# Fused attention, top-1 experts and gated feed-forward: a rare-case branch moved behind the feed-forward, the limits in one transfer, more TensorE fillers, another VectorE order

## The chip, the cores and the metric

The kernel runs on one core of a Trainium2 chip. The metric is the device time of one execution in microseconds (us); each kernel is run several times and the median is given. The engines are TensorE (PE in the profile; PEld is its weight load), VectorE (DVE), ScalarE (ACT), GpSimd (POOL) and SyncE (SP, which here only issues transfers). A name with q at its end (POOLq) is an engine's instruction sequencer.

## What is computed

Three stages, in float32, on B = 2 sequences of S = 768 tokens, H = 8 heads of D = 64 (cut from the reference):

```python
scores = scale * np.matmul(q, k.transpose(0, 1, 3, 2))
keep = is_sink | in_window             # key < n_sink, or 0 <= query - key < window
a = np.exp(scores - max); a = a / (sum + 1e-09); x = np.matmul(a, v)   # -> x[1536, 512]
logits = xn @ en.T / tau               # both normed; 8 experts
expert_idx = argmax(logits); gate_w = softmax(logits)[expert_idx]
x[mask] = gate_w[mask, None] * (np.maximum(x[mask] @ w1[e], 0.0) @ w2[e])   # F = 1024
out = ((x @ w_a) * (x @ w_b)) @ w_out  # d_ff = 1536
```

`n_sink` is 4 and `window` is 128, both given as 64-bit integers at run time.

## The kernel before

All products are made to float32 accuracy from three float32r products: an operand is split into a high part (a cast on ScalarE or VectorE) and the rest (a subtraction on VectorE), and hi*hi, lo*hi and hi*lo are added in PSUM. The kernel writes its instruction order by hand (`tc.manual_schedule()`): every engine runs its instructions in the order in which the program's lines issue them, and waits where a tile is not ready.

**Start and attention.** SP issues the first halves of q and k, then the two limits (lines 193 and 194, each broadcast to 128 partitions into `ctli`), then the second halves and further loads. VectorE turns the limits into masks (`early_masks`, lines 222 to 229) before it can use the first scores (`sc_exp`, line 474). A loop over g goes through the 12 token tiles, four steps each (one step: two heads): `p_t` transposes the weights of two steps ago, `sc_mm` makes scores (line 459 for the first tile, 465 for the others), `pv` multiplies by v, `back` and what follows finish a tile and route it to an expert. While little real work is there, `warm_pe(n)` issues n transposes of the identity into a PSUM tile that nobody reads (line 964), the fillers: `WARM` = 8 + 4 + 3 ahead of the first scores, and `WARMG[g]` at the end of step g.

**Experts.** Tokens are sorted by expert; weights are loaded by expert and split; items of one or two tiles of tokens run through `mm1`/`mm2` and `pa`/`pb` (lines 708, 780 to 782, 800 to 802) and their results go to `y_d` in DRAM (`ys`, line 768). In the same loop the gate values, the position of every token and the counts `cnt` are worked out a few instructions at a time (`side_gen`), and the feed-forward's weights begin to be decoded.

**The branch.** A plan with a fixed number of slots covers the usual case. If the limits or the counts don't fit it, a general path repairs the result: line 1473 loads a count into a register of each engine, line 1475 compares it, and the repair (a thousand PE instructions) is jumped over when the count is 0, as it is here. The jumped path has a short block of its own, in which every engine waits until its earlier work and transfers are done and raises its semaphores by what the repair would have added. Then comes the feed-forward.

**Feed-forward.** Tokens go in NG = 3 groups of 512, the 1536 hidden units in NF = 12 steps f of 128. For each f, `ab_mms` makes 24 products for a and b (lines 1600 to 1602), `g_split` multiplies them (`asb`, line 1609), splits the result into `gh` (ScalarE, 1612) and `gl` (VectorE, 1613), and `out_mms` makes 12 products into four PSUM tiles (1620 to 1622), one step later. The weights arrive packed and are decoded in 24 halves: `conv_step(m)` casts the high part of half m on ScalarE, and on VectorE prepares half m+1 (`conv_b0`, two operations, lines 1384 and 1385; `conv_b1`, two, lines 1390 and 1391) and subtracts the low part of m (`wl`, line 1401). Four halves are decoded before the first group, the other 20 during its steps f = 0 to 9, one `conv_step` ahead of `g_split` and one behind it:

```python
        ab = ab_mms(f)
        if more:
            conv_step(2 * (f + NF0), f1)
        cur = g_split(f, ab, 'V')
        if more:
            conv_step(2 * (f + NF0) + 1, f1)
```

`done` scales a finished tile and scatters its rows to the output with an indirect transfer from POOL (line 1667). At the program's end (line 1721) SP waits for every transfer, and all engines meet.

Of the kernel before, what the change touches and what calls it, by code (L numbers as in the profile page):

```python
# [20 lines left out]
P = 128  # L21
# [42 lines left out]
WARMG = [6, 3, 4, 1]  # L64
# [38 lines left out]
TINY = 2.0 ** -15 * 1.125  # L103

# [19 lines left out]
def tile_kernel(ctx, tc, q, k, v, n_sink, window, emb, tau, w1, w2, wc, out, dbg=None):  # L124
# [1046 lines left out]
    fe = pool(ctx, "fe", side="right")  # L1171

    def side_gen(w_, pl, psp, tag):
# [172 lines left out]
        V.tensor_copy(cide, cpos[:, 0:4])  # L1346
        G.tensor_scalar(g, g, 1.0 / GSC, None, op0=ALU.mult)
# [16 lines left out]
    wres = {}  # L1364

    raw2, sq2 = {}, {}
# [3 lines left out]
    def load_conv(m):  # L1370
        if m >= NH:
            return
        r = raw2[m] = fe.tile([P, HW, 2], I32, tag="raw", name="raw2", bufs=3)
        nc.sync.dma_start(r.rearrange("p n c -> p (n c)"), wc32[m])

    def conv_abs(m):
        if m < NH:
            sq2[m] = fe.tile([P, HW], F32, tag="sq", name="sq", bufs=2)
            nc.scalar.activation(sq2[m], raw2[m][:, :, 1].bitcast(F32), AF.Abs)  # L1379

    def conv_b0(m):
        if m < NH:
            b, t = sq2[m], sq2[m].bitcast(I32)
            nc.vector.tensor_scalar(b, b, TINY, None, op0=ALU.max)  # L1384
            nc.vector.tensor_scalar(t, t, 5, 2, op0=ALU.logical_shift_left, op1=ALU.logical_shift_right)

    def conv_b1(m):
        if m < NH:
            r, t = raw2.pop(m), sq2[m].bitcast(I32)
            nc.vector.scalar_tensor_tensor(t, r[:, :, 0], 29, t, op0=ALU.logical_shift_right, op1=ALU.bitwise_or)  # L1390
            nc.vector.scalar_tensor_tensor(t, r[:, :, 1], -1073741824, t, op0=ALU.bitwise_and, op1=ALU.bitwise_or)  # L1391

    def conv_step(m, wpool):
        f, h = divmod(m, 2)
        if h == 0:
            wres[f] = (wpool.tile([P, CW], F32R, name=f"wh{f}"), wpool.tile([P, CW], F32R, name=f"wl{f}"))
        wh, wl = (t[:, h * HW:(h + 1) * HW] for t in wres[f])
        sq = sq2.pop(m)
        nc.scalar.copy(wh, sq)
        conv_b0(m + 1)  # L1400
        nc.vector.tensor_tensor(out=wl, in0=sq, in1=wh, op=ALU.subtract)  # L1401
        conv_abs(m + 2)
        conv_b1(m + 1)
        load_conv(m + 4)

    xh2 = fe.tile([P, NP, TG], F32R, name="xh2")
    xl2 = fe.tile([P, NP, TG], F32R, name="xl2")
    ygs = {}

    def gather_y(u, w=None, rows=None):  # L1410
        ygs[u] = w.tile([P, DM], F32, tag="ygn", name="ygn", bufs=4) if w else fe.tile([P, DM], F32, tag="yg", name="yg", bufs=3)
        early = u < 4 and w is None
        nc.gpsimd.indirect_dma_start(out=ygs[u], out_offset=None, in_=y_d[0:rows or (YR0 if early else YR1), :],  # L1413
                                     in_offset=bass.IndirectOffsetOnAxis(ap=(cide if early else cidx)[:, u:u + 1], axis=0))

    def y_t(u, psp, tag):
        yp = psp.tile([P, NP, P], F32, tag=tag, name="yp2")
        for kc in range(NP):
            nc.tensor.transpose(yp[:, kc, :], ygs[u][:, kc * P:(kc + 1) * P], ident)  # L1419
        return yp  # L1420

    def y_s(u, yp):
        tt = u % 4
        ts_ = slice(tt * P, (tt + 1) * P)
        nc.scalar.copy(xh2[:, :, ts_], yp)
        nc.vector.tensor_tensor(out=xl2[:, :, ts_], in0=yp, in1=xh2[:, :, ts_], op=ALU.subtract)
# [46 lines left out]
    ns_v = nc.values_load(cnt[0:1, 0:1], min_val=0, max_val=4 * int(GENF))  # L1473
    mst.close()
    with tc.If(ns_v > 0):  # L1475
# [97 lines left out]
        with ExitStack() as gs:  # L1573
            xw = pool(gs, "xw3")
            xps = pool(gs, "xps3", space=PSUM)
            for u in range(NU):
                gather_y(u, xw, NBLK * P)
                nc.sync.dma_start(y2_d[u * P:(u + 1) * P, :], ygs[u])
            for u in range(NU):
                yc = xw.tile([P, DM], F32, tag="ygn", name="yc", bufs=4)  # L1580
                nc.sync.dma_start(yc, y2_d[u * P:(u + 1) * P, :])
                nc.sync.dma_start(y_d[u * P:(u + 1) * P, :], yc)
            nc.vector.tensor_copy(cidx, tok)
            for u in range(4):
                gather_y(u, xw, YR1)
                y_s(u, y_t(u, xps, "a"))
# [29 lines left out]
    def out_mms(po, f, gh, gl, done=None, tts=range(4)):  # L1616
        wh, wl = wres[f]
        for tt in tts:
# [4 lines left out]
            if done is not None:  # L1623
                done(tt)

    NG = NT // TG
    outs = []
    pend = None
    tail = []
# [95 lines left out]
```

## Time and profile before

| | |
|---|---|
| median of 3 runs | 661.46 us (661.29 to 661.57) |
| the profiled execution, its own time | 659.85 us |
| its span, first to last instruction | 658.0 us |
| PE busy | 628.6 us, 96% of the span |
| PEld busy | 515.4 us, 78% |
| DVE busy | 396.4 us, 60% |
| ACT busy | 304.8 us, 46% |
| POOL busy | 122.2 us, 19% |
| mean granted TensorE clock | 0.977 of full speed |

The page divides the span into 40 slices; in its line for the clock only the first two slices, slice 21, near 335 us, and the last stand clearly below full. The stretches show the same by stage. Busy shares are means over stages with different limits: attention to about 100 us, experts to 329 us, the first feed-forward group to 430 us, the other two to the end. In the timeline a row gives the start in us, the duration in us (of several equal instructions together, with their count), engine, line, operation, the tile written and the tiles read, and in brackets how long the engine had been idle and what ended that.

### The profile page before, as it was taken

How to read it: one execution, taken by the hardware profiler on the slowest of the kernel's cores; microseconds unless marked ns; L12 is line 12 of the kernel's file. 1: busy time of each engine (PE TensorE's matmuls, PEld its weight loads, DVE VectorE, ACT ScalarE, POOL GpSimd, SP SyncE). 2: the span in 40 equal slices, each digit the busy share in tenths (PEclk: the TensorE clock that was granted, in tenths of full speed). 3: DMA queues.
4: the chain of work that ended last, by engine and by line, in shares of the span. 5: the costliest groups of instructions: out<-in, count | busy, mean ns of one | idle time of the engine just before them, and what ended most of it. 6: DMA issues, size and time to landing. Idle time of an engine off the chain costs nothing. (4 is left out here: it accounts for less than half of the span.)

```text
span 658.0 us, 10420 instructions
## 1 busy us (share of the span) xinstructions
PE 628.6 (96%) x3665; PEld 515.4 (78%) x3665; DVE 396.4 (60%) x910; ACT 304.8 (46%) x581; POOL 122.2 (19%) x269
## 2 busy tenths in 40 slices
PE   8999999889999999998969999999999999999995
PEld 5777777779998989887858767678888888888884
DVE  5688878998888766798839999943111113111111
ACT  4678777667575657667524444422111113111111
POOL 7243345481042211020010000004000003000002
PEclk7699999989999999999979999999999999999999
DMA  4244325323787887587253454203000002000001
GB/s 144 85 160 130 130 81 191 147 76 134 254 289 273 269 280 267 180 304 253 86 177 134 154 186 150 96 17 114 0 1 0 1 0 81 0 1 1 0 1 64
DMA packets 25967, 80.77 MB, mean 123 GB/s; under 512 B 3560, under 2 KB 4072, under 8 KB 25904
## 3 DMA queue, kind: packets, MB, share of 16 engines
q1 hardware_dynamic: 22560, 69.23, 31.5%
q0 software_dynamic: 3344, 10.77, 4.8%
q8 instruction: 31, 0.51, 0.3%
q14 instruction: 32, 0.26, 0.1%
HBM read 81.82 MB, written 10.75 MB: 141 GB/s over the span
## 5 line engine op out<-in xcount | busy, mean ns | idle before, releaser
L1600 PE MATMUL pp<-xh,wh 128*128 128x512 f32 x288 | 114.5, 398 | 5.7 <-DVEq L1475 5.7
L1609 DVE TENSOR_TENSOR asb<-pp,asb 128x512 f32<-128x512 f32 x36 | 24.8, 689 | 151.5 <-PE pp L1602 151.5
L1601 PE MATMUL pp<-xl,wh 128*128 128x512 f32 x288 | 114.9, 399 | 0.0
L1602 PE MATMUL pp<-xh,wl 128*128 128x512 f32 x288 | 114.6, 398 | 0.0
L603 DVE TENSOR_TENSOR lo<-raw,hi 128x1024 fp32r<-128x1024 f32 x80 | 96.1, 1228 | 7.9 <-ACT hi L595 6.2
L595 ACT CAST hi<-raw 128x1024 fp32r<-128x1024 f32 x87 | 88.0, 1050 | 7.8 <-PE hp L708 4.1
L1600 PEld LDWEIGHTS pp<-xh,wh 128*128 128x128 f32 x288 | 54.7, 190 | 19.4 <-ACTq L1475 6.2
L1601 PEld LDWEIGHTS pp<-xl,wh 128*128 128x128 f32 x288 | 54.8, 190 | 13.1
L1602 PEld LDWEIGHTS pp<-xh,wl 128*128 128x128 f32 x288 | 54.8, 190 | 12.9
L1612 ACT CAST gh<-asb 128x512 fp32r<-128x512 f32 x36 | 22.3, 620 | 90.2 <-DVE asb L1609 87.4
L1608 ACT COPY asb<-pp 128x512 f32<-128x512 f32 x36 | 21.0, 583 | 89.6 <-PE pp L1602 89.5
L1620 PE MATMUL po<-wh,gh 128*128 128x512 f32 x144 | 57.9, 402 | 3.9 <-ACT gh L1612 3.9
L477 ACT ACTIVATE p<-st,mn 128x260 f32<-128x260 f32 (+1 forms) x96 | 46.6, 487 | 29.2 <-DVE mn L474 22.8
L1622 PE MATMUL po<-wh,gl 128*128 128x512 f32 x144 | 57.6, 400 | 0.0
L1621 PE MATMUL po<-wl,gh 128*128 128x512 f32 x144 | 56.8, 394 | 0.0
L1413 POOL DMA_INDIRECT yg<-y_d,cidx x8 | 8.3, 1040 | 215.6 <-PE yp L1419 187.3
L780 PE MATMUL hT<-pxh,hi 128*128 128x256 f32 x160 | 45.5, 285 | 0.0
L782 PE MATMUL hT<-pxh,lo 128*128 128x256 f32 x160 | 44.7, 280 | 0.0
L781 PE MATMUL hT<-pxl,hi 128*128 128x256 f32 x160 | 44.7, 279 | 0.0
L474 DVE CUSTOM_DVE_ANT_0 st<-sc,m 128x260 f32<-128x260 f32 (+1 forms) x96 | 35.0, 399 | 10.4 <-PE sc L465 5.1
L1379 ACT ACTIVATE sq<-raw 128x768 f32<-128x768 f32 x24 | 22.1, 923 | 39.4 <-DVE wl L1401 39.4
L1613 DVE TENSOR_TENSOR gl<-asb,gh 128x512 fp32r<-128x512 f32 x36 | 24.9, 692 | 24.8 <-ACT gh L1612 24.8
(344 smaller groups left out, 1335.1 us busy)
## 6 DMA issues: line engine op xcount, KB each, us to landing
raw<-in_moe_w_dram SPq DMA_DIRECT2D x88, 512.0 KB
raw<-in_moe_w_dram SPq DMA_DIRECT2D x24, 768.0 KB
y_d<-ys SPq DMA_DIRECT2D x16, 256.0 KB
vt<-in_v_dram SPq DMA_DIRECT2D x12, 256.0 KB
x_d<-xl SPq DMA_DIRECT2D x12, 256.0 KB
qt<-in_q_dram SPq DMA_DIRECT2D x11, 256.0 KB
kt<-in_k_dram SPq DMA_DIRECT2D x10, 256.0 KB
qt<-in_q_dram SPq DMA_DIRECT2D x2, 128.0 KB
```

The costliest lines, as they stand in the source:

```text
L477: nc.scalar.activation(p[:, j, 0:W], st[:, 0:W], AF.Exp, bias=z['mn'][:, h:h + 1], scale=-1.0, accum_out=z['sm'][:, h:h + 1])
L595: ER = {'A': lambda o, i: nc.scalar.copy(o, i), 'V': lambda o, i: nc.vector.tensor_copy(o, i), 'P': lambda o, i: nc.gpsimd.tensor_copy(o, i)}
L603: EL[elo].tensor_tensor(out=lo, in0=raws[g], in1=hi, op=ALU.subtract)
L780: nc.tensor.matmul(hT[:, c, :], lhsT=hi[:, ws], rhs=z['xh'][:, kc, :], start=(c == 0 and kc == 0), stop=False, skip_group_check=True)
L781: nc.tensor.matmul(hT[:, c, :], lhsT=hi[:, ws], rhs=z['xl'][:, kc, :], start=False, stop=False, skip_group_check=True)
L782: nc.tensor.matmul(hT[:, c, :], lhsT=lo[:, ws], rhs=z['xh'][:, kc, :], start=False, stop=(kc == NP - 1), skip_group_check=True)
L1600: nc.tensor.matmul(pp, lhsT=wh[:, ws], rhs=xh2[:, kc, :], start=(kc == 0), stop=False)
L1601: nc.tensor.matmul(pp, lhsT=wh[:, ws], rhs=xl2[:, kc, :], start=False, stop=False)
L1602: nc.tensor.matmul(pp, lhsT=wl[:, ws], rhs=xh2[:, kc, :], start=False, stop=(kc == NP - 1))
L1620: nc.tensor.matmul(po[tt], lhsT=gh[:, ts_], rhs=wh[:, 1024:CW], start=(f == 0), stop=False, skip_group_check=True)
L1621: nc.tensor.matmul(po[tt], lhsT=gh[:, ts_], rhs=wl[:, 1024:CW], start=False, stop=False, skip_group_check=True)
L1622: nc.tensor.matmul(po[tt], lhsT=gl[:, ts_], rhs=wh[:, 1024:CW], start=False, stop=(f == NF - 1), skip_group_check=True)
```

## The change

- The three lines of the limits: the host puts `n_sink` and `window` side by side into one array `limits`, and one transfer, issued first on ACT's queue, fetches it.
- `WARMG` changes, so that 41 fillers instead of 14 stand in the attention steps.
- The branch and the whole general path move behind the feed-forward. The feed-forward becomes a function `ffn_run`, called once in the main path, and a second time (`slow`) inside the general path, which now repeats it. The count is loaded in the third group at f = 2, where a hint for the branch is marked as well. As the main feed-forward now runs before it is known that the plan fits, the gather index for groups two and three is clamped (`cidc`).
- In `conv_step` behind `g_split`, the two operations of `conv_b0(m + 1)` now come ahead of `gl`.

The diff, cut to its core (the moved functions stand in it only where their text changes):

```diff
-WARMG = [6, 3, 4, 1]
+WARMG = [8, 7, 8, 2, 4, 4, 0, 0, 4, 4]
...
+    nc.scalar.dma_start(ctli, lim.bitcast(I32).partition_broadcast(P))
     q0, k0 = new_q(0, 0), new_k(0, 0)
     for a in (0, W2):
         ld(q0, q, 0, 0, a, a + W2)
         ld(k0, k, 0, 0, a, a + W2)
-        if a == 0:
-            nc.sync.dma_start(ctli[:, 0:2], n_sink.bitcast(I32).partition_broadcast(P))
-            nc.sync.dma_start(ctli[:, 2:4], window.bitcast(I32).partition_broadcast(P))
...
         V.tensor_copy(cide, cpos[:, 0:4])
+        yield
+        V.tensor_scalar(cpos[:, 4:NU], cpos[:, 4:NU], 0.0, float(YR1 - 1), op0=ALU.max, op1=ALU.min)
+        V.tensor_copy(cidc, cpos)
...
+        def conv_step(m, wpool, mid=None):
...
             nc.scalar.copy(wh, sq)
             conv_b0(m + 1)
+            if mid:
+                mid()
             nc.vector.tensor_tensor(out=wl, in0=sq, in1=wh, op=ALU.subtract)
...
-    ns_v = nc.values_load(cnt[0:1, 0:1], min_val=0, max_val=4 * int(GENF))
     mst.close()
-    with tc.If(ns_v > 0):
+
+    def ffn_run(z, stack, tag):
...
         def g_split(f, ab, el):
...
             nc.scalar.copy(gh, asb)
-        EL[el].tensor_tensor(out=gl, in0=asb, in1=gh, op=ALU.subtract)
-        return f, gh, gl
+            return f, gh, gl, lambda: EL[el].tensor_tensor(out=gl, in0=asb, in1=gh, op=ALU.subtract)
...
                 ab = ab_mms(f)
+                if not slow and (gi, f) == (NG - 1, 2):
+                    ns.append(nc.values_load(cnt[0:1, 0:1], min_val=0, max_val=4 * int(GENF)))
+                    tc.mark_branch_hint_location("cover", "LikelyTaken")
                 more = gi == 0 and f + NF0 < NF
                 if more:
                     conv_step(2 * (f + NF0), f1)
-            cur = g_split(f, ab, 'V')
+                *cur, low = g_split(f, ab, 'V')
                 if more:
-                conv_step(2 * (f + NF0) + 1, f1)
+                    conv_step(2 * (f + NF0) + 1, f1, low)
+                else:
+                    low()
...
+    ns = []
+    ffn_run(ff, fz, "")
+    fz.close()
+    ns_v = ns[0]
+
+    with tc.If(ns_v > 0, label="cover"):
...
         with ExitStack() as gs:
...
+            ffn_run(ffn_parts(pool(gs, "fes", side="right"), True), gs, "s")
...
+        limits=np.concatenate([np.asarray(a['n_sink']).reshape(1), np.asarray(a['window']).reshape(1)]),
```

How the order of instructions moves, at three places. On PE, at the start of attention (`wps` is the tile of the fillers, `sc` are scores, `tp` transposed weights, `ou` the product with v), before:

```order
L964 MATMUL wps<-ident 128x128 x15
L459 MATMUL sc<-kf,qt 128x128 x2
L964 MATMUL wps<-ident 128x128 x6
L459 MATMUL sc<-kf,qt 128x128 x2
L964 MATMUL wps<-ident 128x128 x3
L490 MATMUL tp<-ident,p 128x128 x2
L459 MATMUL sc<-kf,qt 128x128 x2
L964 MATMUL wps<-ident 128x128 x4
```

and with the change:

```order
L964 MATMUL wps<-ident 128x128 x15
L459 MATMUL sc<-kf,qt 128x128 x2
L964 MATMUL wps<-ident 128x128 x8
L459 MATMUL sc<-kf,qt 128x128 x2
L964 MATMUL wps<-ident 128x128 x7
L490 MATMUL tp<-ident,p 128x128 x2
L459 MATMUL sc<-kf,qt 128x128 x2
L964 MATMUL wps<-ident 128x128 x8
```

The runs of fillers grow; further on, four more stand behind each of steps 4, 5, 8 and 9, where none stood.

On VectorE, around `asb` of a step f of the first group (`sq` is the half that is being decoded, `wl` its low part), before:

```order
L1391 SCALAR_TENSOR_TENSOR sq<-raw_4971,sq 128x768
L1609 TENSOR_TENSOR asb<-pp,asb 128x512
L1613 TENSOR_TENSOR gl<-asb,gh 128x512
L1384 TENSOR_SCALAR sq<-sq 128x768
L1385 TENSOR_SCALAR sq<-sq 128x768
L1401 TENSOR_TENSOR wl_9528<-sq,wh_9527 128x768
```

and with the change:

```order
L1397 SCALAR_TENSOR_TENSOR sq<-raw_5000,sq 128x768
L1522 TENSOR_TENSOR asb<-pp,asb 128x512
L1390 TENSOR_SCALAR sq<-sq 128x768
L1391 TENSOR_SCALAR sq<-sq 128x768
L1526 TENSOR_TENSOR gl<-asb,gh 128x512
L1409 TENSOR_TENSOR wl_5152<-sq,wh_5151 128x768
```

The two operations of `conv_b0` moved from behind `gl` to between `asb` and `gl`; nothing was added.

At the branch, PE's last product of the experts and what follows it, before:

```order
L800 MATMUL yp<-hi,hh 128x512
L801 MATMUL yp<-hi,hl 128x512
L802 MATMUL yp<-lo,hh 128x512
L1473 TENSOR_LOAD cnt
L1475 COMPARE_AND_BRANCH
L1476 COMPARE_AND_BRANCH
```

and with the change, first PE at the same place, then POOL at the end of the third group:

```order
L802 MATMUL yp<-lo,hh 128x512
L1513 MATMUL pp<-xh_2784,wh_4659 128x512
L1514 MATMUL pp<-xl_2785,wh_4659 128x512
L1515 MATMUL pp<-xh_2784,wl_4660 128x512
L1513 MATMUL pp<-xh_2784,wh_4659 128x512
```

```order
L1583 MEMSET warm 128x1
L1584 DMA out_dram<-os__7022,ctok 1536x512
L1583 MEMSET warm 128x1
L1584 DMA out_dram<-os__7032,ctok 1536x512
L1605 COMPARE_AND_BRANCH
L1606 COMPARE_AND_BRANCH
```

The compare left the place between the experts and the feed-forward on every engine, and stands behind the last scatter; the jumped block (on POOL waits for its transfers and a correction of its semaphores) stands behind the general path. No row for a prefetch hint is in the built order outside the two loops of the general path, in either kernel.

## Rows read from the trace of the kernel before

**Rows 1.** Stretches: busy us (count) of PE, PEld, DVE, ACT, POOL; granted clock; DMA.

```profile
10.00:26.00 16.00, 15.85 (x84) 10.83 (x84) 11.12 (x53) 10.68 (x37) 4.02 (x14) 0.50 0.42 133
...
334.70:340.90 6.20, 6.10 (x15) 4.80 (x16) 3.36 (x5) 2.07 (x3) 3.23 (x3) 0.50 0.30 94
343.40:429.60 86.20, 82.98 (x346) 63.77 (x345) 78.69 (x108) 39.72 (x53) 0.00 (x0) 1.00 0.43 145
429.60:649.00 219.40, 218.59 (x955) 176.10 (x954) 46.94 (x69) 40.11 (x67) 14.20 (x23) 1.00 0.05 16
```

**Rows 2.** Timeline at the branch: start us, us, engine, line, operation; idle, releaser.

```profile
329.09 0.58 ACT L595 COPY ys<-yp 128x512 f32<-128x512 f32 x1 [0.81 <-PE yp L802]
...
334.80 0.77 PE L1600 MATMUL pp<-xh,wh 128*128 128x512 f32 x1 [5.74 <-DVEq L1475]
...
340.89 0.40 PE L1602 MATMUL pp<-xh,wl 128*128 128x512 f32 x1
...
342.94 0.39 PE L1602 MATMUL pp<-xh,wl 128*128 128x512 f32 x1
...
343.44 0.69 DVE L1609 TENSOR_TENSOR asb<-pp,asb 128x512 f32<-128x512 f32 x1 [1.94 <-PE pp L1602]
```

**Rows 3.** Line 1475 by sequencer: ns min/median/max, first and last start.

```profile
L1475 POOLq EVENT_SEMAPHORE  x6: 17/30/43, 311.4 to 314.5; - x6
...
L1475 ACTq EVENT_SEMAPHORE  x2: 17/17/17, 334.3 to 334.4; - x2
...
L1475 POOLq COMPARE_BRANCH  x1: 58/58/58, 308.8 to 308.8; - x1
L1475 POOLq INC_SWDGE_SEM  x1: 660/660/660, 314.6 to 314.6; - x1
...
L1475 ACTq COMPARE_BRANCH  x1: 50/50/50, 330.4 to 330.4; - x1
```

**Rows 4.** Timeline of VectorE in one step f of the first group.

```profile
353.01 0.68 DVE L1609 TENSOR_TENSOR asb<-pp,asb 128x512 f32<-128x512 f32 x1
354.45 0.69 DVE L1613 TENSOR_TENSOR gl<-asb,gh 128x512 fp32r<-128x512 f32 x1 [0.76 <-ACT gh L1612]
355.06 0.55 DVE L1384 TENSOR_SCALAR sq<-sq 128x768 f32<-128x768 f32 x1
...
362.65 0.68 DVE L1609 TENSOR_TENSOR asb<-pp,asb 128x512 f32<-128x512 f32 x1
```

**Rows 5.** Chain that ended last, VectorE, last step with a conversion.

```profile
429.61 0.69 DVE asb L1609
```

**Rows 6.** Timeline of the start, VectorE and PE.

```profile
1.53 3.46 PE L964 MATMUL wps<-ident 128*128 128x128 f32 x15 [1.53 <-POOL ident masks.py:199]
...
5.90 0.21 DVE L222 CAST ctl<-ctli 128x4 f32<-128x4 int32 x1 [5.04 <-DMA ctli<-in_window_dram]
...
7.90 0.29 DVE L474 CUSTOM_DVE_ANT_0 st<-sc,m 128x128 f32<-128x128 f32 x1 [0.15 <-DVE m L229]
...
8.88 0.55 PE L964 MATMUL wps<-ident 128*128 128x128 f32 x3
...
10.63 1.11 PE L964 MATMUL wps<-ident 128*128 128x128 f32 x4
```

**Rows 7.** Timeline of PE: score products that open steps of attention.

```profile
14.67 0.59 PE L465 MATMUL sc<-kh,qh 64*128 64x260 f32 x2
...
26.82 0.39 PE L465 MATMUL sc<-kh,qh 64*128 64x260 f32 x2
...
45.03 0.39 PE L465 MATMUL sc<-kh,qh 64*128 64x260 f32 x2
...
54.29 0.39 PE L465 MATMUL sc<-kh,qh 64*128 64x260 f32 x2
```

**Rows 8.** Instructions of the program end, line 1721, by sequencer.

```profile
L1721 POOLq DRAIN  x3: 46/115/4799, 652.4 to 657.8; - x3
L1721 SPq DRAIN  x3: 7/7/13, 656.0 to 657.5; - x3
```

More of the change, by code (lines that the diff above doesn't have):

```diff
@@ L1 @@
 import math
+from types import SimpleNamespace
 from contextlib import ExitStack
@@ L123, in tile_kernel @@
 @with_exitstack
-def tile_kernel(ctx, tc, q, k, v, n_sink, window, emb, tau, w1, w2, wc, out, dbg=None):
+def tile_kernel(ctx, tc, q, k, v, lim, emb, tau, w1, w2, wc, out, dbg=None):
     nc = tc.nc
@@ L1170, in tile_kernel @@
     cide = rt.tile([P, 4], I32, name="cide")
-    fe = pool(ctx, "fe", side="right")
+    cidc = rt.tile([P, NU], I32, name="cidc")
+    fz = ctx.enter_context(ExitStack())
+    fe = pool(fz, "fe", side="right")
     def side_gen(w_, pl, psp, tag):
@@ L1381, in conv_b0 @@
[L1381 to L1414, printed above, removed]
@@ L1428, in tile_kernel @@
+    ff = ffn_parts(fe, False)
+    load_conv, conv_abs, conv_b0, conv_b1, conv_step, gather_y, y_t, y_s = (getattr(ff, x) for x in FFN)
     side = side_gen(rw1, pl, xps, "xp")
@@ L1573, in tile_kernel @@
         with ExitStack() as gs:
[L1574 to L1586, printed above, removed]
-    f1 = pool(ctx, "f1")
-    f2 = pool(ctx, "f2", bufs=2, side="right")
-    fpa = pool(ctx, "fpa", bufs=2, space=PSUM)
-    fpo = pool(ctx, "fpo", space=PSUM)
-    def ab_mms(f):
-        wh, wl = wres[f]
-        ab = []
-        for n in range(2):
-            pp = fpa.tile([P, TG], F32, tag="ab"[n], name="pp")
-            for kc in range(NP):
-                ws = slice(n * 512 + kc * P, n * 512 + (kc + 1) * P)
-                nc.tensor.matmul(pp, lhsT=wh[:, ws], rhs=xh2[:, kc, :], start=(kc == 0), stop=False)
-                nc.tensor.matmul(pp, lhsT=wh[:, ws], rhs=xl2[:, kc, :], start=False, stop=False)
-                nc.tensor.matmul(pp, lhsT=wl[:, ws], rhs=xh2[:, kc, :], start=False, stop=(kc == NP - 1))
-            ab.append(pp)
-        return ab
@@ L1606, in g_split @@
-    def g_split(f, ab, el):
-        asb = f2.tile([P, TG], F32, tag="asb", name="asb", bufs=1)
-        nc.scalar.copy(asb, ab[0])
-        nc.vector.tensor_tensor(out=asb, in0=ab[1], in1=asb, op=ALU.mult)
-        gh = f2.tile([P, TG], F32R, tag="gh", name="gh", bufs=2)
-        gl = f2.tile([P, TG], F32R, tag="gl", name="gl", bufs=2)
-        nc.scalar.copy(gh, asb)
-        EL[el].tensor_tensor(out=gl, in0=asb, in1=gh, op=ALU.subtract)
-        return f, gh, gl
-    def out_mms(po, f, gh, gl, done=None, tts=range(4)):
-        wh, wl = wres[f]
-        for tt in tts:
-            ts_ = slice(tt * P, (tt + 1) * P)
-            nc.tensor.matmul(po[tt], lhsT=gh[:, ts_], rhs=wh[:, 1024:CW], start=(f == 0), stop=False, skip_group_check=True)
-            nc.tensor.matmul(po[tt], lhsT=gh[:, ts_], rhs=wl[:, 1024:CW], start=False, stop=False, skip_group_check=True)
-            nc.tensor.matmul(po[tt], lhsT=gl[:, ts_], rhs=wh[:, 1024:CW], start=False, stop=(f == NF - 1), skip_group_check=True)
-            if done is not None:
-                done(tt)
@@ L1683 @@
-_INS = ['q', 'k', 'v', 'n_sink', 'window', 'moe_expert_emb', 'moe_tau', 'moe_w1', 'moe_w2', 'moe2_w']
+            ffn_run(ffn_parts(pool(gs, "fes", side="right"), True), gs, "s")
+_INS = ['q', 'k', 'v', 'limits', 'moe_expert_emb', 'moe_tau', 'moe_w1', 'moe_w2', 'moe2_w']
 def _laid_out(np, a):
```

223 lines of the change are left out of this document (150 added, 73 removed).

## The prediction

> **What bounds the kernel now.** I read the page's slices first, then the stretches by stage, then the timelines at the places that the change touches. Three stretches show what counts. In the first group of tokens of the feed-forward VectorE is busy 78.69 of 86.20 us at a granted clock of 1.00, and the steps repeat VectorE's own order; in the two groups after it TensorE is busy 218.59 of 219.40 us and nothing else matters [rows 1]. So time taken out ahead of the last conversion step comes out of the end, one for one, and after it only TensorE's work counts. Two stretches run at the lower of the two clock levels, 1.2 GHz: 10 to 26 us in attention, and 334.7 to 340.9 us right behind the branch [rows 1].
>
> Attention and the routed experts hand their time on: the weight loads wait for routing results, not for a clock on the wall, so I count an earlier start there in full.
>
> **The branch ahead of the feed-forward.** TensorE gets its first product at 334.80, after 5.74 us of waiting for VectorE's branch code; the last operation it really needs, ACT's copy of `ys`, ends at 329.09 + 0.58 = 329.67 [rows 2]. In the built order the first product now waits for that copy alone, as its PSUM bank is reused. So 334.80 - 329.67 = 5.1 us go. The pause also brought the clock down: 14 starts from 334.80 to 340.89 are 0.435 us apart, the 9 behind them to 342.94 are 0.228 apart [rows 2]. The 23 intervals of the first `ab_mms` took 8.14 us; at 0.228 they take 5.24, since a gap of 0.7 us is left where nearly 6 stood. That is 2.9 us. Together **-8.0 us**, and `asb` of step 0, which ends the wait [rows 2], moves by it. VectorE's conversion ahead of it sets no later limit: it now runs beside TensorE's 5.2 us. Bounds: 7.5 (a slow first product or two) to 8.2.
>
> **The VectorE step.** One step of the first group is a fixed string of twelve VectorE operations. Between `asb` and `gl` VectorE waits 0.76 us for ACT's `gh`; `asb` to `gl` takes 1.44 us where an operation that waits for nothing hands on after 0.61 (`gl` to the next) [rows 4]. The change puts two conversion operations there, whose inputs ACT finished a half step before. Nine steps from 343.44 to 429.61 are 9.57 us each [rows 2, 5]. This one is 362.65 - 353.01 = 9.64, so in the mean step `asb` to `gl` takes 0.07 less, 1.37. Behind `asb` the next operation can start after 0.61 to 0.68, its duration [rows 4]. So a step loses between 1.37 - 0.68 = 0.69 and 1.44 - 0.61 = 0.83. I take 0.72, near the lower end, which belongs to the mean step: **-6.5 us**, bounds 6.2 to 7.5. What is late next: `gl` now ends 0.61 + 2 x 0.55 + 0.69 = 2.4 us after `asb` started, where it ended after 1.44 + 0.69 = 2.1 [rows 4], and the third output product of TensorE waits for it. TensorE has 36 products of 0.228, 8.2 us, in a step of 8.85, so 0.3 us more of waiting fits, and some 0.3 are left.
>
> **The branch at the end.** It is not gone but moved. ACT's branch code began 334.3 - 330.4 = 3.9 us after its compare, POOL's 311.4 - 308.8 = 2.6 us after [rows 3]; I read this as fetching code from elsewhere. The change marks a hint, but the built order has no prefetch row at that line (the only such rows stand in two loops of the rare path), so I count the branch as unhinted. Who is exposed: SP reaches its compare long before the end, as its last load is that of a weight tile; TensorE's queue runs ahead; VectorE and ACT end before POOL. POOL issues the last scatter, and its drain at the end runs from 652.4 for 4.8 us, to 657.2, while SP is through with all other waits at 656.0 [rows 8]. A fetch of 2.6 to 3.9 us from 652.5 lies inside that drain. Behind it come the waits for the scatters and the semaphore correction, 0.66 us [rows 3]. I take **+0.7 us**. Bounds: 0 (all inside the drain) and +3.3 (POOL's fetch of 2.6 behind the drain instead of beside it, then 0.66).
>
> **The start.** VectorE waits for the limits until 5.90 and reaches the first masked scores at 7.90 [rows 6]. The limits were two transfers, third and fourth on SP's queue; now one goes out first on ACT's queue. The first fillers end at 1.53 + 3.46 = 4.99 [rows 6] and the scores come behind them, about half a microsecond later, so the gain is at most 2.4 us; at least it is 0. More fillers then stand in front of the next scores on TensorE, which is in order, so I take the middle, -1.3 us. SP's later loads move up by two issues; nothing waits for them there, 0.
>
> The fillers: 14 become 41, behind the first 15. From row to row, 15 took 3.46 us and 4 took 1.11, so (3.46 - 1.11) / 11 = 0.21 for one more; three at 8.88 took 0.55, where that pace would give 1.11 - 0.21 = 0.90 [rows 6]. So the pace rose to the upper level between 4.99 and 8.88, and then, with TensorE often waiting, fell to 0.50 for 10 to 26 us [rows 1]. Four steps of attention took 26.82 - 14.67 = 12.15 us there, and take 54.29 - 45.03 = 9.26 us at 1.00 [rows 7]. If the level holds, -2.9 us. The fillers cost TensorE 27 times some 0.11 (half of 0.21), 3.0 us, much of it in waits; of the 16 in later steps, where it is busier, I put half on the path, +0.9. Together **-3.3 us**. Bounds: -5.3 (2.4 and 2.9, the fillers free) to -1.2 (-1.3 and -2.9 with all 3.0 us on the path).
>
> What speaks against this term is a rule: by the Trainium skill, TensorE: Matmul & The Clock Gate, Part 4: PE-mode transpose, the full clock does not engage for transposes, and the fillers are transposes. By it the sum would lose the 2.9 us. The trace disagrees so far: up to 8.88 TensorE ran 21 such fillers and eight small score products, and the pace rose.
>
> Smaller edits: two VectorE operations clamp the gather index (at most 0.2 us each, by the 0.21 of a cast [rows 6]), off the chain; the register load late in the third group reads a count that was ready when POOL compared at 308.8 [rows 3]. Both 0; 0.4 is the upper bound.
>
> **Sum.** -8.0 - 6.5 + 0.7 - 3.3 = -17.1 us against the profiled execution of 659.85 us, so 642.7. The median of the runs, 661.46, stands 1.6 us above that execution; the same change gives **644.4 us**.
>
> **Rivals.**
> - The clock falls at the start all the same. For it: 16 us at 0.50 although fillers stood there already, and the new ones stop at places. Against: the pace rose behind the first fillers [rows 6]. Then -1.3 from the limits stays, and 16 fillers at 0.21, half exposed, cost 1.7: +0.4 where I have -3.3, **648.1 us**. This is also what the rule on transposes above would give.
> - The branch at the end is exposed in full, +3.3 instead of +0.7: **647.0 us**. For it: no hint row in the built order. Against: POOL's drain covers it [rows 8]. The Trainium skill, Runtime: NRT & Kernel Launch, section Instruction fetch mechanics, is on its side: a taken branch to code outside the fetched pages waits for a fetch by DMA before anything runs. The 3.9 us of ACT agree with it; what covers the wait it does not say.
> - The reordered step pays half, because TensorE's wait for the later `gl` takes over: 0.36 a step, 3.2 instead of 6.5, **647.7 us**. Against: the 0.3 us that are left to TensorE in each step.
> - Slower than before: those longer waits for `gl` bring the clock down in the first group. A step is then 36 products of 0.435, 15.7 us instead of 8.85; it decides as soon as more than two and a half of the nine steps run so (2.5 x 6.85 is the 17.1 gained); with all nine, 644.4 + 61.6 = **706 us**. Against: TensorE waited longer per step before, at 1.00 [rows 1].
>
> **How the numbers follow.** Forecast 0.52; the clock at the start 0.19; the end 0.12; the step 0.10; two of these three at once, 650.3 to 651.4 us, 0.05; the slow step 0.02. My forecast's bounds, all added up, are 640.5 and 650.3 (with 0.4 for the smaller edits); they will hardly all fall to one side, and its own likely range is 642 to 646.5. A range of 641.8 to 648.8 takes in the three single rivals and leaves out the last two and the corners, some 0.15. Within 0.2%, about 1.3 us, is what a measurement of this kernel can tell from no change; only a mix of the last case falls there or above. Faster 0.97, same 0.01, slower 0.02.
>
> **What would show it.** Right: the first `pp` within 1 us of the last `ys` copy and 0.228 us between products at once; steps of 8.8 to 8.9 us and no VectorE wait for `gh` in them; granted clock 1.00 from 10 to 26 us and four steps in some 9.3 us; first masked scores near 6 us; POOL's last scatter to the end of the span at most 1.5 us longer than now. Wrong: 0.50 behind 10 us, steps over 9.2 us, or a compare on POOL with over 4 us to its next instruction and nothing behind it.

## The result and the profile after

The changed kernel takes **644.08 us** (median of 4 executions, 643.75 to 645.05) where the kernel before took 661.38 in the same job (4 executions, 660.43 to 661.57): a ratio of 0.9744, 95% interval 0.9727 to 0.9761. The profiled execution took 643.75 us, 16.1 less than that of before, and its span is shorter by the same 16.1 us. Four marks that stand in both traces divide it:

| from | to | before, us | after, us | difference |
|---|---|---|---|---|
| start | last product of the experts (L802) | 328.66 | 324.16 | -4.50 |
| that | `asb` of step 0 | 14.78 | 6.92 | -7.86 |
| that | `asb` of step 9, the last conversion | 86.17 | 79.14 | -7.03 |
| that | first scatter of the last group | 219.16 | 218.86 | -0.30 |
| that | end of the span | 9.23 | 12.82 | +3.59 |

The page's first line and its clock line in 40 slices (tenths of full speed):

```profile
span 641.9 us, 10457 instructions
...
PEclk9999999989999999999999999999999999999997
```

The low slices at the start and near 335 us are gone. Two stand below full: the last, in which TensorE's work ends, and the ninth. (In the kernel before the ninth stood at 8 too, and the last at 9; the text ahead of the prediction counts the last among its low ones and not the ninth.) The stretches say where the ninth loses (columns as in [rows 1]):

```profile
10.00:26.00 16.00, 14.63 (x133) 10.67 (x132) 13.24 (x62) 10.89 (x37) 5.62 (x18) 1.00 0.42 133
...
136.00:144.00 8.00, 6.36 (x41) 6.36 (x42) 7.19 (x8) 4.45 (x7) 2.15 (x4) 0.79 0.39 99
```

The first of these stretches stood at 0.50 in [rows 1]. In the timeline of the start, VectorE and PE, the rows that answer to [rows 6] and [rows 7]:

```profile
3.83 0.50 DVE L222 CAST ctl<-ctli 128x4 f32<-128x4 int32 x1 [2.98 <-DMA ctli<-in_limits_dram]
...
6.52 0.29 DVE L474 CUSTOM_DVE_ANT_0 st<-sc,m 128x128 f32<-128x128 f32 x1 [0.15 <-DVE m L229]
```

```profile
12.83 0.50 PE L465 MATMUL sc<-kh,qh 64*128 64x260 f32 x2 [0.49 <-DVE mn L474]
...
21.82 0.39 PE L465 MATMUL sc<-kh,qh 64*128 64x260 f32 x2
...
31.35 0.39 PE L465 MATMUL sc<-kh,qh 64*128 64x260 f32 x2
```

The masked scores come 1.38 us earlier, and the score product of step 4 comes 1.84 earlier than the 14.67 of [rows 7]. The four steps from 12.83 take 8.99 us in place of 12.15; the four behind them, with the last eight fillers among them, take 9.53 where the trace of before has 8.92 (26.82 to 35.74).

Where the branch stood, and the VectorE step (they answer to [rows 2] and [rows 4]):

```profile
324.60 0.59 ACT L595 COPY ys<-yp 128x512 f32<-128x512 f32 x1 [0.82 <-PE yp L802]
...
325.24 0.50 PE L1513 MATMUL pp<-xh,wh 128*128 128x512 f32 x1 [0.68 <-ACT ys L595]
```

```profile
339.94 0.68 DVE L1522 TENSOR_TENSOR asb<-pp,asb 128x512 f32<-128x512 f32 x1
340.54 0.55 DVE L1390 TENSOR_SCALAR sq<-sq 128x768 f32<-128x768 f32 x1
341.12 0.56 DVE L1391 TENSOR_SCALAR sq<-sq 128x768 int32<-128x768 int32 x1
341.60 0.69 DVE L1526 TENSOR_TENSOR gl<-asb,gh 128x512 fp32r<-128x512 f32 x1
...
348.72 0.68 DVE L1522 TENSOR_TENSOR asb<-pp,asb 128x512 f32<-128x512 f32 x1
```

TensorE now waits 0.68 us for the last copy of `ys` and for nothing else. The wait of 0.76 us for `gh` is filled, and a step takes 8.78 us.

The end is what got longer. Line 1605, the branch, by sequencer, and the drains of the program's end (they answer to [rows 3] and [rows 8]):

```profile
L1605 POOLq EVENT_SEMAPHORE  x6: 17/30/43, 635.9 to 636.3; - x6
...
L1605 PEldq COMPARE_BRANCH  x1: 3522/3522/3522, 627.5 to 627.5; - x1
...
L1605 POOLq COMPARE_BRANCH  x1: 58/58/58, 633.1 to 633.1; - x1
L1605 POOLq INC_SWDGE_SEM  x1: 1060/1060/1060, 636.4 to 636.4; - x1
```

```profile
L1745 POOLq DRAIN  x3: 46/109/3586, 637.5 to 641.7; - x3
L1745 SPq DRAIN  x3: 7/7/13, 638.2 to 641.4; - x3
```

POOL compares at 633.1, has its next instruction at 635.9, raises its queue's semaphore until 637.5, and only then drains, for 3.59 us. In the kernel before the drain started right behind the last scatter.

### The profile page after: what moved, and what is told of

It reads as the page before. It is cut to its first block, busy times and chain, and to the rows that moved or that the text cites. A ratio compares the mean times of both kernels' runs of the same rounds, so it can differ in the third digit from the quotient of the medians.

```text
span 641.9 us, 10457 instructions
## 1 busy us (share of the span) xinstructions
PE 618.1 (96%) x3692; PEld 511.7 (80%) x3692; DVE 397.3 (62%) x912; ACT 304.6 (47%) x581; POOL 116.0 (18%) x269
## 4 chain that ended last, share of the span: by engine, by line
PE 69%; issue 17%; DVE 7%; ACT 3%; POOL 2%; DMA 0%; POOLq 0%; DVEq 0%; ACTq 0%
PE pp L1513 7%; PE pp L1514 7%; PE pp L1515 7%; PE hp L708 5%; PE po L1534 3%; PE po L1532 3%; PE po L1533 3%; PE ou L521 3%; PE hT L782 3%; PE hT L780 3%; PE hT L781 3%; PE yp L800 3%; PE yp L802 3%; PE yp L801 3%; PE sc L465 2%
## 5 line engine op out<-in xcount | busy, mean ns | idle before, releaser
L1514 PE MATMUL pp<-xl,wh 128*128 128x512 f32 x288 | 113.6, 394 | 0.0
L780 PE MATMUL hT<-pxh,hi 128*128 128x256 f32 x160 | 45.4, 284 | 0.0
L1421 POOL DMA_INDIRECT yg<-y_d,cidc x8 | 7.6, 951 | 201.0 <-PE yp L1426 174.5
```

Of the source, the lines that this page charges most:

```text
L780: nc.tensor.matmul(hT[:, c, :], lhsT=hi[:, ws], rhs=z['xh'][:, kc, :], start=(c == 0 and kc == 0), stop=False, skip_group_check=True)
L1514: nc.tensor.matmul(pp, lhsT=wh[:, ws], rhs=xl2[:, kc, :], start=False, stop=False)
```

## The experiments

Twelve kernels, each timed beside the kernel before on the same chip, and with a profile. Executions of one kernel differ here by up to 6 us, and mostly with their mean granted clock: the quickest executions of the kernel before, at 656.0 to 656.5 us, all have 0.987, and most others 0.971 to 0.982. Four others, at 0.987 to 0.990, took 658.5 to 661.6, so the mean clock does not tell all of it. The changed kernel itself was timed in the first job only, four times; the median of the kernel before was 661.38 us there and 659.68 to 660.50 in the later jobs. So a difference of a microsecond between medians of two jobs shows little, and each timed result stands beside marks of the profiled execution, which don't depend on what the clock did elsewhere.

### The branch at the end

**No branch.** Cut:

```diff
-    with tc.If(ns_v > 0, label="cover"):
...
```

> The changed kernel without its conditional block at the end: the path for other counts of tokens is left out. Theory (the branch is paid in full at the end): the queue drain of GpSimd starts right behind the last scatter, as in the kernel before, instead of behind the block; the start of the last scatter to the end of the span falls from 8.54 us to 5.4, and the time from 644.1 to about 640.9 (640.4 to 641.4). Rival (the recorded term: drain and transfer of the last tile cover most of the branch): 643.4, with the 3.16 us coming from something else at the end.

Measured: 640.17 us (638.81 to 642.62); against before 0.9713 (0.9678 to 0.9748). First scatter to end of span: 638.4 - 629.10 = 9.30 us, as before the change (9.23). POOL's drain in this kernel:

```profile
L1644 POOLq DRAIN  x3: 46/109/4842, 632.7 to 638.1; - x3
```

It starts right behind the scatters again. The branch at the end costs what the balance shows, some 3.5 us, not 0.7.

**A short block.**

```diff
     with tc.If(ns_v > 0, label="cover"):
-        with tc.If(ns_v >= int(GENF)):
...
         with ExitStack() as gs:
             xw = pool(gs, "xw4")
...
             for b in range(YR1 // P, NBLK):
                 nc.sync.dma_start(y_d[b * P:(b + 1) * P, :], zg)
-        for x, n0, n1 in ((1, NSS, E), (0, NPS, NPOS - 1)):
...
-            ffn_run(ffn_parts(pool(gs, "fes", side="right"), True), gs, "s")
```

> The changed kernel with the conditional block cut to one memset and its copies of zeros into the working buffer: the condition is read and tested as before, the path for other counts of tokens is left out. Theory A (the price is the fetch of code that lies far behind the block): the 2.8 to 3.5 us between the compare and the next instruction shrink to under 1 us, and the time comes near that without the branch, 641 to 642. Theory B (the price is the test and the meeting of the engines, whatever the length of the block): the compare still takes 2.8 us and more, and the time stays at 643.7 to 644.3.

Measured: 640.16 us (638.70 to 641.54), 0.9704 (0.9671 to 0.9736); first scatter to end 9.22 us. Line 1605 in this kernel:

```profile
L1605 PEldq COMPARE_BRANCH  x1: 223/223/223, 627.6 to 627.6; - x1
...
L1605 POOLq COMPARE_BRANCH  x1: 50/50/50, 632.7 to 632.7; - x1
L1605 POOLq EVENT_SEMAPHORE  x1: 17/17/17, 632.9 to 632.9; - x1
```

Test and branch are the same, and cost nothing that shows: 0.2 us from POOL's compare to its next instruction, where the long block took 2.8. That the long wait goes with a fetch of code can be read from the transfers: from 627 to 637.5 us the changed kernel has two queues that bring in instructions (queue, packets, MB, share of 16 engines), and this kernel has none in that stretch.

```profile
q14 instruction: 6, 0.05, 1.6%
q8 instruction: 2, 0.03, 1.3%
```

Theory A holds so far, but this block skips no software transfer either. The next two kernels part the two.

**A short block with gathers; the long block without.**

```diff
+            for u in range(4):
+                zg = xw.tile([P, DM], F32, name=f"zg{u}")
+                nc.gpsimd.indirect_dma_start(out=zg, out_offset=None, in_=y_d[0:YR0, :], in_offset=bass.IndirectOffsetOnAxis(ap=cide[:, u:u + 1], axis=0))
+                nc.sync.dma_start(y_d[(YR1 // P + u % 2) * P:(YR1 // P + u % 2 + 1) * P, :], zg)
```

> The short conditional block of the run before, with four gathers of GpSimd's software queue and their stores in it instead of the memset; the path for other counts of tokens is left out. Theory A (distance of the jump is the price): as with the short block, 640.2 (639.8 to 640.8). Theory C (skipping software DMAs is the price: the queue's semaphore is raised for the skipped ones, 1.06 us in the changed kernel, and the drain takes its 3.6 us anew behind it): the instruction that raises the semaphore is back, the drain starts behind it, and the time is 641.5 to 643.5.

```diff
-        xg = gather_x(gather_ix(c_src, h + 1, w), h, w)
+        gather_ix(c_src, h + 1, w)
+        xg = w.tile([P, DM], F32, tag="xg", name="xg", bufs=XGB)
+        nc.sync.dma_start(xg, x_d[0:P, :])
...
+            if slow:
+                nc.sync.dma_start(ygs[u], y_d[u * P:(u + 1) * P, :])
+                return
...
+                if slow:
+                    nc.sync.dma_start(out[u * P:(u + 1) * P, :], os_)
+                    return
```

> The changed kernel with the whole conditional block at its length, but GpSimd's gathers and scatters in it replaced by plain transfers on the synchronous queue, so the path for other counts of tokens computes something else. Theory A (distance): the 2.8 to 3.5 us behind each compare stay and the time is 643.4 to 644.2. Theory C (skipped software DMAs): nothing raises the queue's semaphore, the drain ends when the last scatter is processed, 4.6 us after its start, and the time is 640.2 to 641.5. If both have a share, it lies between.

Measured: short with gathers 640.39 us (638.86 to 640.53), 0.9714 (0.9681 to 0.9747), first scatter to end 9.42; long without 642.60 us (640.78 to 644.11), 0.9748 (0.9712 to 0.9783), first scatter to end 11.48. From the short block with gathers, then from the long one without (line of the branch, line of the end):

```profile
L1605 POOLq INC_SWDGE_SEM  x1: 1061/1061/1061, 633.2 to 633.2; - x1
```

```profile
L1652 POOLq DRAIN  x3: 46/103/3588, 634.3 to 638.4; - x3
```

```profile
L1613 POOLq EVENT_SEMAPHORE  x2: 17/17/17, 636.1 to 636.2; - x2
...
L1613 PEldq COMPARE_BRANCH  x1: 3462/3462/3462, 627.6 to 627.6; - x1
...
L1613 POOLq COMPARE_BRANCH  x1: 57/57/57, 633.4 to 633.4; - x1
```

```profile
L1753 POOLq DRAIN  x3: 46/109/3586, 636.3 to 640.4; - x3
```

Theory C alone falls: the semaphore correction is back in the short block and costs 0.2 us at the end. Theory A alone falls too: the long block without software transfers is between. The drains tell why. Without a branch POOL's drain takes 4.84 us, and ends 4.6 us after the last scatter starts; started later, in three kernels and at three distances, it takes 3.59. So the correction of 1.06 us, on the heels of the scatter, hides in a drain that lasts to about that time anyway. Behind a fetch of 2.7 us nothing hides: fetch, correction and a drain that still takes 3.59 run in a row. By first scatter to end, 2.2 us of the 3.5 are the distance (11.48 - 9.30) and 1.3 the software transfers (12.82 - 11.48). About half a microsecond of the distance's share stands ahead of all this: the last `os` on ACT starts at 632.40 where without a branch it starts at 631.93, and the last scatter with it. The trace names VectorE's branch code as its releaser; that was not tried.

### The VectorE step and the branch ahead of the feed-forward

```diff
+                low()
                 if more:
-                    conv_step(2 * (f + NF0) + 1, f1, low)
-                else:
-                    low()
+                    conv_step(2 * (f + NF0) + 1, f1)
```

> The changed kernel with the two conversion operations back behind gl, the order of the kernel before. Theory (VectorE's wait between asb and gl sets each of the nine steps): asb comes every 9.57 us in place of 8.79, the first matmul group of the feed-forward ends 7.0 us later, and the time is 651.1 (650.2 to 651.9). Rival (part of the 7 us belongs to the branch that stood ahead of the steps before, not to their order): the pitch lies between, 9.2 us, and the time is 647 to 648.

Measured: 651.22 us (651.08 to 652.91), 0.9892 (0.9858 to 0.9926): 7.1 above the changed kernel. `asb` of step 0 stands at 331.10 here and at 331.08 there; the last of the nine steps, in VectorE's timeline:

```profile
407.90 0.68 DVE L1522 TENSOR_TENSOR asb<-pp,asb 128x512 f32<-128x512 f32 x1
409.27 0.69 DVE L1526 TENSOR_TENSOR gl<-asb,gh 128x512 fp32r<-128x512 f32 x1 [0.69 <-ACT gh L1525]
...
417.47 0.68 DVE L1522 TENSOR_TENSOR asb<-pp,asb 128x512 f32<-128x512 f32 x1
```

The pitch is 9.57 us again, the wait for `gh` is back, and nine steps take 86.37 us in place of 79.14. The order alone is worth 7.2 us, and all of it reaches the end.

The kernel before, without its branch:

```diff
-    ns_v = nc.values_load(cnt[0:1, 0:1], min_val=0, max_val=4 * int(GENF))
     mst.close()
-    with tc.If(ns_v > 0):
...
```

> The kernel before without its conditional block: the path for other counts of tokens is left out, and nothing else is changed. Theory (gap and half clock at the branch, measured as 7.9 us between the two traces, belong to the branch alone): the first product of the feed-forward starts within 1 us of the last copy of ys and runs at a pitch of 0.228 us, and the time falls from 660.5 or 661.4 to 652.6 to 653.5. Rival (a part of the gap is the wait for the last gathers, which moved with other edits): 654.5 to 656.

Measured: 651.78 us (647.68 to 653.82), 0.9876 (0.9835 to 0.9917), 8.5 below the kernel before in the same job. The executions spread widely, and how much of that comes from the start is not shown; the profiled one, the slowest, has the clock at 0.50 there again. The place itself is clear:

```profile
329.97 0.40 PE L802 MATMUL yp<-lo,hh 128*128 128x512 f32 x1
...
330.40 0.59 ACT L595 COPY ys<-yp 128x512 f32<-128x512 f32 x1 [0.82 <-PE yp L802]
...
331.04 0.50 PE L1487 MATMUL pp<-xh,wh 128*128 128x512 f32 x1 [0.68 <-ACT ys L595]
```

With `asb` of step 0 at 336.88, the stretch from the last L802 takes 6.91 us, where it took 14.78 with the branch and takes 6.92 in the changed kernel. So the branch alone cost 7.87 us.

### The start

**Old fillers.**

```diff
-WARMG = [8, 7, 8, 2, 4, 4, 0, 0, 4, 4]
+WARMG = [6, 3, 4, 1]
```

> The changed kernel with the old table of fillers, 14 transposes in four steps in place of 41 in eight. Theory (the fillers hold the clock): the granted clock is about 0.50 again in 10 to 26 us, four steps there take 12 us in place of 9.0, the last 8 fillers are saved (about 0.6 us), so 646.0 to 647.2. Rival 1 (the earlier limits alone keep the clock up, transposes count for nothing): the clock stays at 1.00 and the time is 643.0 to 643.8.

Measured: 646.55 us (642.22 to 646.74), 0.9785 (0.9748 to 0.9821). The stretch from 10 to 26 us in this kernel (0.68, where the theory had about 0.50):

```profile
10.00:26.00 16.00, 14.79 (x91) 10.37 (x92) 10.75 (x51) 9.82 (x32) 3.81 (x14) 0.68 0.43 133
```

The score products of steps 4, 8 and 12 stand at 12.86, 24.87 and 34.09: step 4 as early as in the changed kernel, then 12.01 us for four steps instead of 8.99, then 9.22 instead of 9.53. So in these two executions the fillers bring 3.0 us and cost 0.3 (the 9.22 begin at the lower clock still; the next kernel gives the cost alone). Two of the six executions took 642.2 and 643.9, at a higher mean clock: the fall does not come every time. Nor do the 41 fillers always prevent it: two of the kernels that keep them and the early limits (the long block without software transfers above, the one with 18 more fillers below) had 0.89 over 10 to 26 us when profiled. This is also the test of the rule in the Trainium skill, TensorE: Matmul & The Clock Gate, Part 4: PE-mode transpose, by which transposes do not bring the full clock. Nothing but transposes differs between these two kernels, and the clock of the stretch is 0.68 in one and 1.00 in the other; the measurement, one profile of each, decides against the rule here.

**Fewer fillers.**

```diff
-WARMG = [8, 7, 8, 2, 4, 4, 0, 0, 4, 4]
+WARMG = [8, 7, 8, 2, 4, 4]
```

> The changed kernel without the eight fillers of the steps with indices 8 and 9. Theory (they are paid in full, since TensorE has no wait there): the stretch of those steps is 0.6 us shorter, the clock stays at 1.00 in 10 to 60 us, and the time is 643.3 to 643.6. Rival (they hold the clock in some executions): the clock falls in 20 to 30 us, and the time is 644.5 to 646.

Measured: 645.45 us (641.89 to 646.42), 0.9783 (0.9751 to 0.9815). The profiled execution is the fastest of the six, with the clock at 1.00 from 0 to 330 us, and there step 12 is reached 0.59 us earlier (30.76 for 31.35). The other five took 643.55 to 646.42, four of them at a mean clock of 0.985 to 0.988 against its 0.995. So the theory priced the eight fillers rightly, and the rival's median is what came. Where the clock fell in those four was not profiled, so that these eight fillers hold it is not shown.

**The limits.** Both kernels put them back on SP's queue behind the first halves of q and k, in one transfer and in two:

```diff
-    nc.scalar.dma_start(ctli, lim.bitcast(I32).partition_broadcast(P))
...
+        if a == 0:
+            nc.sync.dma_start(ctli, lim.bitcast(I32).partition_broadcast(P))
```

> The changed kernel with the one transfer of the limits put back on the synchronous queue behind the first halves of q and k, where the two transfers of the kernel before were. Theory (the limits are worth what the first masked score is earlier, 1.38 us, or less, since one transfer is issued in place of two): the first masked score near 7.2 to 7.9 us, the clock still 1.00 in 10 to 26 us, 644.8 to 645.5. Rival (the fillers alone do not hold the clock when the first masks come late): the clock falls to 0.50 in that stretch and the time is 647 to 648.5.

```diff
+            nc.sync.dma_start(ctli[:, 0:2], lim[0:1].bitcast(I32).partition_broadcast(P))
+            nc.sync.dma_start(ctli[:, 2:4], lim[1:2].bitcast(I32).partition_broadcast(P))
```

> The changed kernel with the limits in two transfers on the synchronous queue, behind the first halves of q and k, as in the kernel before; the fillers and all else stay. Theory (it is the second transfer that makes the limits late: one transfer in the same place gave the first masked score at 6.49 us): the conversion to ctl waits until about 5.9 us, the first masked score stands at 7.9 us, and the time is 645 to 646 (1.4 us of delay, less what the fillers cover). Rival (number and place of the transfers do not matter, the first execution is limited by the tables of q and k): 6.5 us and 643.9 to 644.2.

Measured: one transfer 643.88 us (642.36 to 646.84), 0.9768 (0.9733 to 0.9803); two 645.15 us (644.50 to 646.94), 0.9786 (0.9755 to 0.9818). VectorE in the one, then in the other:

```profile
4.32 0.17 DVE L223 CAST ctl<-ctli 128x4 f32<-128x4 int32 x1 [3.47 <-DMA ctli<-in_limits_dram]
...
6.49 0.29 DVE L475 CUSTOM_DVE_ANT_0 st<-sc,m 128x128 f32<-128x128 f32 x1 [0.15 <-DVE m L230]
```

```profile
6.68 0.24 DVE L224 CAST ctl<-ctli 128x4 f32<-128x4 int32 x1 [5.83 <-DMA vsr<-in_v_dram]
...
8.71 0.29 DVE L476 CUSTOM_DVE_ANT_0 st<-sc,m 128x128 f32<-128x128 f32 x1 [0.15 <-DVE m L231]
```

My theory of the first fell and its successor held: it is the second transfer that makes the limits late, not the queue or the place. One transfer on SP gives the masked score at 6.49, no later than ACT's 6.52. (Two give it at 8.71, later than the 7.90 of the kernel before; both slices are of one array here, and what the 0.8 us are was not tried. The row names a load of v, issued on the same queue behind the limits, as what ended the wait, so how the second transfer delays the data is not shown.) How much of the 1.27 us between the two medians is the masks and how much the clock, six executions each don't tell: in the profiled ones the clock fell in part in both, to 0.79 (one transfer) and 0.90 (two) over 10 to 26 us, where the changed kernel's held.

### A better version

The ninth slice of the changed kernel is the one other place ahead of the end where the clock falls. PE there:

```profile
135.34 0.28 PE L708 MATMUL hp<-hi,xh 128*128 128x256 f32 x1
137.64 0.38 PE L708 MATMUL hp<-hi,xlo 128*128 128x256 f32 x1 [2.02 <-DVE xlo L672]
...
140.47 0.41 PE L708 MATMUL hp<-hi,xlo 128*128 128x256 f32 x1
140.68 0.41 PE L708 MATMUL hp<-lo,xh 128*128 128x256 f32 x1
```

Some 0.9 us after a wait of 2.02 us has ended, products begin to come 0.21 us apart in place of 0.12.

```diff
+    wp2 = ps_t.tile([P, P], F32, tag="t", name="wp2")
+    for _ in range(18):
+        nc.tensor.transpose(wp2, ident, ident)
     for g in range(4):
         mm1(1, g)
```

> The changed kernel with 18 more fillers at the one other place where its granted clock falls: TensorE waits 2.02 us for xlo at 135.4 to 137.6 us, and from about 138.5 to 142 us the trace shows the half clock, some 14 products at 0.21 us in place of 0.12. Theory (a wait filled with transposes holds the clock there too): clock 1.00 in 136 to 144 us, first product of the second expert as early as before, 1.3 to 1.5 us saved, 642.6 to 642.9. Rival (transposes of this kind do not hold the clock, and what held it at the start was the earlier masks): the clock falls as before, 644.0 to 645.5.

Measured: 643.49 us (642.48 to 644.30), 0.9751 (0.9720 to 0.9781). The stretch and the row behind the fillers:

```profile
136.89 2.13 PE L1161 MATMUL wp<-ident 128*128 128x128 f32 x18
138.77 0.36 PE L708 MATMUL hp<-hi,xh 128*128 128x256 f32 x1
139.18 0.39 PE L708 MATMUL hp<-hi,xlo 128*128 128x256 f32 x1
```

This execution reached the place 1.5 us later, as the clock had fallen at the start (0.89 over 10 to 26 us), and reached the next kind of product as the changed kernel did (first L780 at 145.78, and at 145.76 there). That the 18 fillers won the 1.5 us back it does not show: the long block without software transfers, which has none here (its lines stand two further on), came as late after the same fall at the start, and its clock held as well:

```profile
139.07 0.39 PE L710 MATMUL hp<-hi,xlo 128*128 128x256 f32 x1 [2.02 <-DVE xlo L674]
139.30 0.28 PE L710 MATMUL hp<-lo,xh 128*128 128x256 f32 x1
...
145.67 0.28 PE L782 MATMUL hT<-pxh,hi 128*128 128x256 f32 x1
```

Both reach `asb` of step 0 at 331.16. The five kernels that kept the clock at the start without the 18 fillers and with the 41 of the start (the changed kernel, no branch, the two short blocks, the old order) lost it at this wait, and reach `asb` of step 0 at 331.08 to 331.16 too: an execution lost some 1.5 us in one place or in the other. Without the eight late fillers, and without these 18, the profiled one lost it in neither, and is there at 328.98. With the 18 fillers the executions split in two, three at 642.5 to 642.8 and three at 644.1 to 644.3. So the last run added four fillers where the start still had waits:

```diff
-WARMG = [8, 7, 8, 2, 4, 4, 0, 0, 4, 4]
+WARMG = [8, 7, 8, 6, 4, 4, 0, 0, 4, 4]
```

> The kernel with the 18 fillers at the second wait, and four more in the step with index 3 of the start (6 in place of 2), ahead of TensorE's three short waits of 0.25, 0.49 and 0.31 us at 11.7 to 13.7 us, behind which the clock fell for part of 14.5 to 19 us in the profiled execution of that kernel. Theory (those waits decide whether the clock falls there): the clock is 1.00 in 10 to 26 us and in 136 to 144 us, nearly all executions lie at 642.4 to 643.0, as the three best of that kernel did. Rival (the four fillers only push the transposes of the probabilities back by 0.2 to 0.4 us, and the clock falls in some executions as before): a median of 643.3 to 644.3.

Measured: **642.52 us** (642.33 to 642.65, five executions) with 659.68 for the kernel before in its job, a ratio of 0.9748 (0.9723 to 0.9773). Its stretches:

```profile
10.00:26.00 16.00, 14.87 (x137) 11.09 (x136) 13.27 (x62) 10.90 (x37) 5.58 (x18) 1.00 0.40 133
...
136.00:144.00 8.00, 8.00 (x70) 7.88 (x68) 8.00 (x9) 6.13 (x9) 4.50 (x4) 1.00 0.39 98
```

All five executions lie within 0.32 us, all below the lowest of the changed kernel (643.75, in another job), and the profiled one reaches `asb` of step 0 at 329.59, 1.49 us earlier. The four fillers cost nothing that shows: steps 4, 8 and 12 open at 12.85, 21.83 and 31.35. This version beats the kernel before. That it beats the changed kernel rests on these marks and on the spread, since the two were never timed in one job and their ratios to the kernel before are alike (0.9748 and 0.9744). The quick kind of execution was not new: of the 24 of the four kernels that vary the branch at the end, 7 were some 1.4 us quicker than most of the rest. With the fillers in both waits it came five times in five, on one chip. With the branch out of the way of the end another 3.5 us could be had; how to keep the general path and not pay for jumping over it was not found. Whether a prefetch of the jump's target would do it stays open: the mark that the change sets led to no prefetch row in the built order, so none ran and its worth was not tried.

## Why the prediction was right, point by point

- **The total.** 644.4 forecast, 644.08 measured. It is partly luck: against the profiled execution the sum said -17.1 and the balance is -16.1, and of the terms two were too small by 1.7 together and one by 2.9 the other way. Another 0.3 us went in the groups behind the conversion, for which no term stood. The rest of the match is the step from the profiled execution to the median: 1.6 us before, 0.3 after.
- **The branch ahead of the feed-forward**, -8.0: -7.86 between the traces, -7.87 when the branch alone is cut. Both parts of the term stood: the first product starts 0.05 us after the last copy of `ys` ends, and the products are 0.23 us apart from the second one on.
- **The VectorE step**, -6.5: -7.03 between the traces, -7.2 by the experiment, inside the bounds. I took 0.72 a step where it is 0.78. The mean step's 1.37 from `asb` to `gl` was right (407.90 to 409.27 in the old order); what I took off it was an operation's duration of 0.68, where the next one follows after 0.60 (339.94 to 340.54), and 1.37 - 0.60 is 0.77. `gl` ends 2.35 us behind the start of `asb`, as worked out, and no wait of TensorE took over, so that rival and the slow step fall.
- **The start**, -3.3: -4.50. The limits were put at -1.3 and brought 1.4 at the masks and 1.84 at step 4; their mechanism was read from the wrong end, since the queue does not matter and the second transfer does. The clock's -2.9 measured -3.0 to -3.2. The fillers' +0.9 was 0.6 for the last eight; the cost of the others was not parted from what they bring. The rival in which the clock falls anyway did not come for the changed kernel (1.00 in its profile), but the clock is not safe: it fell in part with all 41 fillers too, to 0.89 in two other kernels with the same start. And my reading that the pace of the first fillers shows the clock has no support in the clock column, which has 1.00 from 1.5 to 5 us, where they stand 0.21 us apart.
- **The branch at the end**, +0.7: this step failed. It measures +3.59 us from the first scatter on, just over my upper bound of 3.3, and "at most 1.5 us longer" was missed with 3.16. The price of the fetch was right (2.8 us on POOL, for my 2.6 to 3.9), that of the correction too low (1.06 for 0.66); what failed was the cover. I wrote that the fetch "lies inside that drain", as if the drain ran while POOL fetched. It is an instruction of POOL's own queue, behind the branch, and takes 3.59 us even when it starts long after the scatter. The rival of the exposed branch had the right size for this term with a chance of 0.12; its time, 647.0, did not come because the step and the start gave more. The rule that stood beside it, in the Trainium skill, Runtime: NRT & Kernel Launch, section Instruction fetch mechanics, agrees with the runs: the long block costs 2.7 (POOL) to 3.7 us (SP) behind a compare, the short one at most 0.2.

## What to carry to other kernels

A branch that jumps over a long block costs a fetch (here 2.7 to 3.7 us on an engine), and next to nothing when the block is short (0.2 us at most); moved to the end it is cheaper here than ahead of TensorE's work (3.6 for 7.9 us), but it is hidden only by what another engine does meanwhile, never by an instruction that stands behind it in the same queue. Ask of every cover in whose queue it stands. And where several executions of one kernel differ, look for stretches in which the clock fell behind a short wait: with 22 transposes put into two waits, all five executions here were of the quick kind, and the profiled one came to the feed-forward 1.5 us earlier.

## What was not expected of the hardware

- POOL's drain at the end takes 3.59 us (3.586, 3.586, 3.588 in three kernels), whether it starts 4.1, 2.6 or 1.2 us behind the start of the last scatter; with nothing of note between scatter and drain it takes 4.6 to 4.8.
- Two broadcast transfers of 1 KB in a row made the masks 2.2 us later than one of 2 KB in the same place (8.71 and 6.49 us).
- Whether the clock falls at the start differs between executions of one program (0.89 and 1.00 in profiles of kernels that are the same up to there). The same kernel before took from 656.01 to 662.12 us over the jobs of this study; with fillers in both waits five executions lie within 0.32 us.
